# First batch's attention in one fixed order on three engines, with other counts of zero products and earlier raw weight words

## The chip, the core and the metric

The kernel runs on one core of one Trainium2 chip. The metric is the device time of one execution in microseconds (us), taken as the median of three runs. The engines are called as in the profile: PE is TensorE (matrix products), PEld its weight loads, DVE is VectorE, ACT is ScalarE, POOL is GpSimd, SP is SyncE, whose queue issues every DMA here.

## What is computed

The reference, cut to what matters, is a masked attention followed by two feed-forward blocks, all in float32 or better:

```python
scores = scale * np.matmul(q, k.transpose(0, 1, 3, 2))      # batch 4, heads 8, seq 576, head_dim 64
...
scores = np.where(masks[None, :, :, :], scores, -1000000000.0)   # window 32, or 128 with every 4th key
scores = scores - np.max(scores, axis=-1, keepdims=True)
attn = np.exp(scores)
attn = attn / (np.sum(attn, axis=-1, keepdims=True) + 1e-09)
x = np.matmul(attn, v)                                       # then 2304 tokens x 512
...
x = (x @ w_a) * (x @ w_b) @ w_out                            # 512 -> 1536 -> 512
h = x @ w_in                                                 # 512 -> 2048
return (np.maximum(h, 0.0) + alpha * np.minimum(h, 0.0)) @ w_out2
```

The weights come as float64 words.

## The kernel before, in words

**Steps.** The program is written as a row of steps. `step(products)` runs what the table `before` holds for this step, then the given products, then what the table `after` holds, then `convey()`, which moves every weight job on by one stage, then loads that were put off (`behind`). The steps are only the order in which the code is written. A scheduler then orders each engine's instructions, and may move one ahead of another that waits; only instructions given to `keep_in_program_order` hold their order, among them the DMA issues.

**The first batch.** Steps 0 to 16 (`n_start` = 17) are the attention of the first batch, one group of two heads and 192 queries for each of the steps 0 to 11. Group i has `scores` (PE into a bank `sp_i`), `largest` (DVE), `exps` (ACT), `weights` (DVE: sum, reciprocal, multiplication), `transposed` (PE into `tp_i`), `moved` (ACT copies `tp_i` to SBUF), `values` (PE into `ap_i`) and `placed` (ACT rounds `ap_i` into `xh`, DVE writes the rest into `xl`; what belongs to later token tiles is copied by DVE). `sp` has two banks, `tp` and `ap` one each.

**Zero products.** `heat(n)` issues n products of 128x512 zeros into a bank that nobody reads: 11 at the start, one in steps 0 to 2, and one in each of the steps 6 to 13.

**Weights.** A job of `convert` loads 512 KB of raw float64 words (`load_raw`, four places), waits two steps, makes float32 of them (two ACT instructions, L188 and L189, then one of DVE, L192, a step later) and splits the result into two parts another step later (`split`: ACT L266, DVE L269). Jobs are written here as a and the block and half (a00, a01, a10, a11, a20, a21, a30) for `w_a` and `w_b`, and o0, o1 for `w_out`. They begin at steps 5, 7, 9, 11, 13, 15 and then at every step from 17.

**The first feed-forward block.** From step 17 on, each block f of 128 hidden columns has three steps: `contract` into `pa` (12 products of 128x512), `contract` into `pb` (12 more), and the products of the block before with `w_out` into `accA`. Block 0 has banks `pa` and `pb`, block 1 the two called `acc`, block 2 `pa` and `pb` again. From step 20 on, groups of the second batch are put between these steps; their scores and values share banks called `sa`, and their queries and keys come by `load_qk(12)` and so on.

Of the kernel before, what the change touches and what calls it, by code (L numbers as in the profile page):

```python
# [62 lines left out]
def tile_kernel(ctx: ExitStack, tc: tile.TileContext, qk, v, mask, wab, wo1, w2, alpha, out):  # L63
# [143 lines left out]
    def convert(src, dest, then=None, raws=raw_ring, places=cf_ring):  # L207
# [7 lines left out]
        if then:  # L215
            then(f)
# [56 lines left out]
    def job_w(k, f, j):  # L273
        def dest():
            if j == 0:
                ws[f] = ws_places[f]
            return ws[f][:, 2 * j], ws[f][:, 2 * j + 1]

        def then(x):
            store_later(4 if now[0] < n_start else 2, wad[f, :, j * 512:(j + 1) * 512], x)  # L280

        queue.append((k, convert(wab[f, j], dest, then)))

    def job_o(k, f):
# [7 lines left out]
        queue.append((k, convert(wo1[f], dest, then)))  # L292
# [28 lines left out]
    class Group:  # L321


        def __init__(self, b, i, k=None, lag=None, tags=None):
# [5 lines left out]
            if k is None:  # L330
                return
            at_step(before, k, self.scores)
            at_step(after, k + lag[0], self.largest)
            at_step(after, k + lag[1], self.exps)
            at_step(after, k + lag[2], self.weights)
            at_step(before, k + lag[3], self.transposed)
            at_step(after, k + lag[3], self.moved)
            at_step(before, k + lag[4], self.values)
            at_step(after, k + lag[4], self.placed)
# [85 lines left out]
        def placed(self):  # L425

            base, p0, n = self.b * S, self.g * GS * QT, GS * QT
            if self.pr < 2:
                segs = [(0, n, base + p0, 1)]
            else:  # L430
                segs, p = [], p0
                while p < p0 + n:
                    r, m = divmod(p, NCLS)
                    e = min(p0 + n, (r + 1) * NCLS)
                    segs.append((p - p0, e - p, base + DILATION * m + r, DILATION))
                    p = e
            for o, n, t0, hop in segs:
                while n:
                    t = max(i for i, (first, _) in enumerate(TILES) if first <= t0)
                    k = min(n, (TILES[t][0] + TILES[t][1] - t0 + hop - 1) // hop)  # L440
                    c0 = t0 - TILES[t][0]
                    to, x = (slice(None), self.pr, slice(c0, c0 + (k - 1) * hop + 1, hop)), self.ap[:, o:o + k]
                    if t:
                        nc.vector.tensor_copy(xn[t][to], x)
                    else:
                        nc.scalar.copy(xh[to], x)
                        nc.vector.tensor_tensor(out=xl[to], in0=x, in1=xh[to].bitcast(F32), op=ALU.subtract)
                    o, n, t0 = o + k, n - k, t0 + k * hop
            self.ap = None
# [42 lines left out]
    def contract(acc, wh, wl, xh, xl, n):  # L492
        for c in range(NC):
            mm3(acc[:, :n], wh[:, c * 128:(c + 1) * 128], wl[:, c * 128:(c + 1) * 128],
                xh[:, c, :n], xl[:, c, :n], c == 0, c == NC - 1)
# [33 lines left out]

    nc.sync.dma_start(out=mk[:, 0:2], in_=mask[:, 0:2])  # L530
    load_qk(0)
# [19 lines left out]
    k = 5  # L551
    while due:
        job = min((x for x in due if n_start + x[1] <= k), default=None)
        if job:
            due.remove(job)
            if job[2] == "a":
                job_w(k, *job[3:])
            else:
                job_o(k, job[3])
        k += 2 if k < n_start else 1  # L560
# [198 lines left out]
    for t, (t0, n) in enumerate(TILES[:N_PLAIN]):  # L759
# [3 lines left out]
        for f in range(NFA):  # L763
# [5 lines left out]
            pa = bank("acc2" if early else "pa")  # L769
# [3 lines left out]
            step(lambda: contract(pa, wf[:, 0], wf[:, 1], xh, xl, n))  # L773
            pb = bank("acc3" if early else "pb")
# [3 lines left out]
            step(lambda: contract(pb, wf[:, 2], wf[:, 3], xh, xl, n))  # L778
# [7 lines left out]
            prev = (accs, wo_of(t, f), box, n, f, NFA, x1d, t)  # L786
        step(flush)
# [391 lines left out]
```

## Time and profile before

| what | us |
|---|---|
| median of three runs | 873.22 |
| lowest and highest of them | 872.21, 873.32 |
| the profiled execution | 876.13 |
| its span, first to last instruction | 874.4 |
| PE busy in the span | 862.3 (99%) |
| DVE busy, ACT busy | 622.0 (71%), 531.5 (61%) |
| mean granted clock of PE | 0.994 |

The span is the part of the profiled execution that the trace covers; the execution around it took 1.7 us more. A granted clock of 1.00 is 2.4 GHz, 0.50 is 1.2 GHz. PE is busy nearly all the time, so a change of the total can come from the stretches in which it is idle, works on what nobody reads, or has the lower clock.

### The profile page before, as it was taken

The page shows a single profiled execution, that of the slowest core. Times are in us where ns is not written, and L with a number is a line of the kernel's source. Part 1 is how long each engine was busy: PE and PEld are TensorE (multiplying, and loading weights), DVE is VectorE, ACT ScalarE, POOL GpSimd, SP SyncE. Part 2 cuts the span into 40 slices and gives each one's busy share as a digit, 9 for nine tenths or more (in the row PEclk, how much of TensorE's full clock was granted, in tenths as well). Part 3 has the DMA queues.
Part 4 walks back from the last instruction along what each step waited for, and adds up shares of the span by engine and source line. Part 5 has one row for each costly group of instructions (what it writes and reads, how often), then busy time and mean ns, then how long its engine had stood idle before and what let it go on. Part 6 is the DMA issues. An engine that isn't in the chain of part 4 may idle for free.

```text
span 874.4 us, 15617 instructions
## 1 busy us (share of the span) xinstructions
PE 862.3 (99%) x5417; PEld 782.1 (89%) x5422; DVE 622.0 (71%) x1438; ACT 531.5 (61%) x1183; POOL 0.7 (0%) x6
## 2 busy tenths in 40 slices
PE   8899999999999999999999999999999999999998
PEld 5578887888887888889999999999999999999998
DVE  5687674547657578969798737898575896557954
ACT  6798884556556566655553637775565855565542
POOL 0000000000000000000000000000000000000000
PEclk9799999999999999999999999999999999999999
DMA  9799984578789788999564559888887787788875
GB/s 256 232 326 358 321 291 156 195 247 276 238 311 324 260 288 278 324 319 316 195 229 167 179 218 312 263 237 263 277 252 240 251 270 225 227 250 258 270 223 184
DMA packets 106397, 225.28 MB, mean 258 GB/s; under 512 B 12112, under 2 KB 27216, under 8 KB 106320
## 3 DMA queue, kind: packets, MB, share of 16 engines
q1 hardware_dynamic: 106320, 224.30, 78.8%
q8 instruction: 43, 0.70, 0.3%
q14 instruction: 34, 0.28, 0.1%
HBM read 172.87 MB, written 51.38 MB: 256 GB/s over the span
## 4 chain that ended last, share of the span: by engine, by line
PE 91%; DMA 4%; DVE 2%; ACT 1%; issue 0%; SPq 0%; ACTq 0%; DVEq 0%
PE acc L1088 20%; PE at L795 12%; PE pb L795 8%; PE pa L795 8%; PE accA L488 4%; PE accA L489 4%; PE accA L490 4%; PE pb L488 4%; PE pa L488 4%; PE pb L490 4%; PE pb L489 4%; PE pa L490 4%; PE pa L489 4%; DMA wsd<-rt 2%; PE sa L416 2%; PE tp L403 2%
## 5 line engine op out<-in xcount | busy, mean ns | idle before, releaser
L269 DVE TENSOR_TENSOR rt<-ft,rt 128x512 fp32r<-128x512 f32 (+3 forms) x191 | 133.5, 705 | 78.7 <-ACT rt L266 77.8
L1088 PE MATMUL acc<-rt 128*128 128x384 f32 x1008 | 187.6, 334 | 0.0
L266 ACT CAST rt<-ft 128x512 fp32r<-128x512 f32 (+3 forms) x191 | 119.8, 633 | 97.6 <-DMA wsd<-rt 31.4
L1088 PEld LDWEIGHTS acc<-rt 128*128 128x128 f32 x1008 | 175.8, 188 | 0.4 <-ACT ft L1071 0.4
L795 PE MATMUL at<-rt 128*128 128x384 f32 x414 | 84.3, 335 | 0.0
L811 ACT COPY ft<-at 128x384 f32<-128x384 f32 x105 | 49.7, 474 | 51.9 <-PE at L795 51.4
L795 PEld LDWEIGHTS at<-rt 128*128 128x128 f32 x414 | 72.7, 188 | 0.4 <-ACT ft L811 0.3
L192 DVE SCALAR_TENSOR_TENSOR ft<-ft 128x512 uint32<-128x512 uint32 x68 | 46.7, 687 | 24.2 <-ACT ft L188 15.5
L488 PE MATMUL accA<-rt 128*128 128x512 f32 (+1 forms) x160 | 62.1, 391 | 0.6 <-DMA rt<-wod 0.6
L387 ACT ACTIVATE ft<-ft 128x96 f32<-128x96 f32 x144 | 52.3, 365 | 16.1 <-DVE ft L374 15.9
L489 PE MATMUL accA<-rt 128*128 128x512 f32 (+1 forms) x160 | 61.7, 386 | 0.0
L490 PE MATMUL accA<-rt 128*128 128x512 f32 (+1 forms) x160 | 61.5, 384 | 0.0
L269 DVE TENSOR_TENSOR rt<-gx,rt 128x768 fp32r<-128x768 f32 x43 | 41.1, 956 | 22.6 <-ACT rt L266 22.3
L189 ACT ACTIVATE ft<-ft 128x512 uint32<-128x512 uint32 x68 | 45.5, 672 | 18.8 <-DMA ft<-in_w 18.6
L795 PE MATMUL pb<-rt 128*128 128x384 f32 x276 | 55.8, 336 | 0.0
L795 PE MATMUL pa<-rt 128*128 128x384 f32 x276 | 55.3, 334 | 0.0
L795 PEld LDWEIGHTS pb<-rt 128*128 128x128 f32 x276 | 48.1, 188 | 1.1 <-DVE gx L808 0.5
L266 ACT CAST rt<-gx 128x768 fp32r<-128x768 f32 x43 | 36.0, 837 | 21.3 <-PE acc L1088 17.0
L795 PEld LDWEIGHTS pa<-rt 128*128 128x128 f32 x276 | 48.6, 188 | 0.0
L795 PE MATMUL at<-rt,rx 128*128 128x384 f32 x216 | 43.9, 336 | 1.6 <-ACT ft L811 1.6
L188 ACT ACTIVATE ft<-ft 128x512 f32<-128x512 f32 x68 | 45.2, 669 | 0.2
L266 ACT CAST rx<-ft 128x512 fp32r<-128x512 f32 (+1 forms) x58 | 32.4, 575 | 14.3 <-DVE ft L715 4.5
(148 smaller groups left out, 1705.1 us busy)
## 6 DMA issues: line engine op xcount, KB each, us to landing
rt<-wsd SPq DMA_DIRECT2D x318, 256.0 KB, 3.2
wsd<-rt SPq DMA_DIRECT2D x112, 256.0 KB, 4.8
ft<-in_w SPq DMA_DIRECT2D x32, 512.0 KB, 5.6
rt<-wod SPq DMA_DIRECT2D x31, 512.0 KB, 4.8
ft<-in_wab SPq DMA_DIRECT2D x24, 512.0 KB, 5.5
ft<-in_qk SPq DMA_DIRECT2D x48, 208.0 KB, 5.3
rx<-wod SPq DMA_DIRECT2D x17, 512.0 KB, 5.0
ft<-in_v SPq DMA_DIRECT2D x48, 144.0 KB, 5.4
```

Of the source, the lines that this page charges most:

```text
L188: held(nc.scalar.activation(f, high.bitcast(F32), AF.Prelu, scale=2.0 ** -112, alpha=-2.0 ** 32))
L189: nc.scalar.activation(low, low, AF.Copy, scale=0.933 * 2.0 ** -29)
L192: nc.vector.scalar_tensor_tensor(out=fi, in0=fi, scalar=3, in1=low, op0=ALU.logical_shift_left, op1=ALU.bitwise_or)
L266: hi_eng.copy(hi, x)
L269: lo_eng.tensor_tensor(out=lo, in0=x, in1=hi.bitcast(F32), op=ALU.subtract)
L387: nc.scalar.activation(self.et[:, s], self.st[:, s], AF.Exp, bias=self.sm[:, 0, s:s + 1], scale=-1.0, accum_out=self.sm[:, 1, s:s + 1])
L488: nc.tensor.matmul(acc, lhsT=wh, rhs=rh, start=first, stop=False)
L489: nc.tensor.matmul(acc, lhsT=wh, rhs=rl, start=False, stop=False)
L490: nc.tensor.matmul(acc, lhsT=wl, rhs=rh, start=False, stop=last)
L795: nc.tensor.matmul(acc[:, :HT], lhsT=a, rhs=x[:, b, c], start=start and c == k == 0, stop=c == 1 and k == 2, skip_group_check=not start,)
L811: nc.scalar.copy(out, acc[:, :HT])
L1088: nc.tensor.matmul(acc[a][:, :HT], lhsT=u, rhs=q[:, b, i % 2], start=new and first and k == 0, stop=last and k == 2, skip_group_check=not new,
```

## The change

Seven edits. (1) A function walks over the instructions of the stretch from the first zero product to the end of block 1's third step, and gives PE, ACT and DVE each an ordering dependence on the instruction written before it: within that stretch these three engines run in the order of the code. (2) The attention's stages are registered so that in step k PE has `sp_k`, `tp_(k-2)`, `ap_(k-3)`, in this order, and then the step's products. (3) `tp` and `ap` have two banks each. (4) Zero products: 5 at the start, 1 and 3 in steps 0 and 1, and 2 in each of the steps 2 to 11. (5) Block 0's `contract` is begun in steps 12 to 14, for the three quarters of the contraction that are there by then; steps 17 and 18 keep the last quarter. (6) Eight jobs instead of six begin before step 17, at other steps, and each has its own number of steps (`lead`) between the load and L188. (7) The first load is `load_qk(0)`, ahead of the mask; `placed` issues its ACT part for all pieces before the DVE part; the float weights are stored 3 steps after the split instead of 4.

```diff
-        yield
-        yield
+        for _ in range(lead):
+            yield
         for f in float_of(raw, places):
...
-            self.tags = tags
+            self.tags = [("at", 2), ("acc%d" % (3 * (i % 2)), 1), ("acc%d" % (1 + i % 2), 1)]
...
+    load_qk(0)
     nc.sync.dma_start(out=mk[:, 0:2], in_=mask[:, 0:2])
-    load_qk(0)
...
-    lag = (0, 0, 1, 2, 3)
-    for i in range(NC * NG):
-        Group(0, i, i, lag, [("at", 2), ("acc0", 1), ("acc1", 1)])
+    first = [Group(0, i) for i in range(NC * NG)]
+    stages = [(after, "largest", 0), (after, "weights", 1), (after, "moved", 2), (after, "placed", 3)]
+    stages += [(before, "scores", 0), (before, "transposed", 2), (before, "values", 3), (after, "exps", 0)]
...
-    k = 5
+    k, starts = 0, [(5, 2), (7, 2), (9, 4), (11, 3), (12, 3), (14, 2), (15, 2), (16, 2)]
     while due:
+        k, lead = starts.pop(0) if starts else (max(k + 1, n_start), 2)
...
-        k += 2 if k < n_start else 1
...
-    heat(11)
+    def in_source_order(first):
+
+        order = mybir.DependencyInfo(mybir.DependencyClass.NoSync, mybir.DependencyReason.DATA)
+        engines, last = [nc.tensor.engine, nc.scalar.engine, nc.vector.engine], {}
+        for n, ins in enumerate(nc.cur_bb.bb.instructions):
+            if n >= first and ins.engine in engines and ins.engine in last:
+                tc.add_manual_dep(ins, last[ins.engine].name, order, reason="in_source_order")
+            last[ins.engine] = ins
...
+        contract(begun[j], ws[0][:, 2 * j], ws[0][:, 2 * j + 1], xh, xl, 512, cs)
+
+    begins = len(nc.cur_bb.bb.instructions)
+    heat(5)
     for k in range(n_start):
-        if k < 3:
-            step(lambda: heat(1))
+        if k < 12:
+            step(lambda: heat((1, 3)[k] if k < 2 else 2))
+        elif k < 15:
+            step(lambda: [begin(*x) for x in (((0, 0),), ((0, 1),), ((0, 2), (1, 0, 1, 2)))[k - 12]])
         else:
-            step(lambda: heat(6 <= k < 14, tc.keep_in_program_order))
+            step()
...
+            cs = [NC - 1] if started else range(NC)
...
+            if (t, f) == (0, 1):
+                in_source_order(begins)
```

Three places show what that does to the order of instructions. Lines L349, L392 and L405 of the changed kernel are L360 (`scores`), L403 (`transposed`) and L416 (`values`) of the kernel before; L481 to L483 are L488 to L490 (`contract`), L268 is L269, L363 and L383 to L385 are L374 and L394 to L396.

PE at the end of the first batch, before (`sa_0` and `sa_1` are the scores of the second batch's first two groups, `pa` is block 0):

```order
L416 MATMUL ap_8_432<-ft 64x64 x6
L360 MATMUL sa_0_590<-ft 64x96 x3
L403 MATMUL tp_10_480<-ident,ft 96x128 x3
L568 LDWEIGHTS zeros
L568 MATMUL pb<-zeros 128x512
L360 MATMUL sa_0_590<-ft 64x96 x2
L488 MATMUL pa<-rt 128x512
L360 MATMUL sa_0_590<-ft 64x96
L489 MATMUL pa<-rt 128x512
L416 MATMUL ap_9_473<-ft 64x64 x6
```

PE at the same place in the changed kernel:

```order
L392 MATMUL tp_10_480<-ident,ft 96x128 x3
L405 MATMUL ap_9_484<-ft 64x64 x6
L481 MATMUL pa<-rt 128x512
L482 MATMUL pa<-rt 128x512
L483 MATMUL pa<-rt 128x512
L392 MATMUL tp_11_507<-ident,ft 96x128 x3
L405 MATMUL ap_10_511<-ft 64x64 x6
```

The second batch's scores were mixed with the end of the first batch; now the first batch ends with block 0's products between its groups, then come the rest of block 0 (18 products), all of `sa_0` and `sa_1`, and block 1.

DVE around the `weights` of group 11, before (`ap_8` is written by L447 and L444, the split of a weight job is L269):

```order
L447 TENSOR_TENSOR rt<-ap_8_432,rt 128x32
L444 COPY ft<-ap_8_432 128x16
L394 TENSOR_SCALAR ft<-ft 128x3
L447 TENSOR_TENSOR rt<-ap_8_432,rt 128x128
L444 COPY ft<-ap_8_432 128x16
L395 RECIPROCAL ft<-ft 128x3
L269 TENSOR_TENSOR rt<-ft,rt 128x512
L396 TENSOR_TENSOR ft<-ft 128x288
```

The same place in the changed kernel:

```order
L441 TENSOR_TENSOR rt<-ap_8_451,rt 128x32
L439 COPY ft<-ap_8_451 128x16
L441 TENSOR_TENSOR rt<-ap_8_451,rt 128x128
L439 COPY ft<-ap_8_451 128x16
L268 TENSOR_TENSOR rt<-ft,rt 128x512
L383 TENSOR_SCALAR ft<-ft 128x3
L384 RECIPROCAL ft<-ft 128x3
L385 TENSOR_TENSOR ft<-ft 128x288
```

The last three rows, the `weights` of group 11, now stand as one piece behind the split of job a01.

SP's queue where the second batch's queries and keys (`in_qk`) begin, before (`in_wab` and `in_wo` are raw words, `wad` is the store of float weights):

```order
L204 DMA ft<-in_wab 128x512
L314 DMA ft<-in_qk 128x416
L199 DMA wad<-ft 128x512
L204 DMA ft<-in_wo 128x512
L314 DMA ft<-in_qk 128x416 x2
L199 DMA wad<-ft 128x512
L204 DMA ft<-in_wab 128x512
L319 DMA ft<-in_v 96x384
```

The same place in the changed kernel:

```order
L199 DMA wad<-ft 128x512
L204 DMA ft<-in_wo 128x512
L313 DMA ft<-in_qk 128x416
L204 DMA ft<-in_wab 128x512
L313 DMA ft<-in_qk 128x416
L204 DMA ft<-in_wab 128x512
L313 DMA ft<-in_qk 128x416
L204 DMA ft<-in_wo 128x512
```

The second and third `in_qk` of the second batch stood right behind o0's load; now the loads of a21 and a30 stand ahead of them.

## Rows read from the trace of the kernel before

**Rows 1.** The page, its first line.
```profile
span 874.4 us, 15617 instructions
```

**Rows 2.** Windows: busy time of each engine, granted PE clock, DMA share, GB/s.
```profile
25.00:30.00 5.00, 3.29 (x29) 2.16 (x31) 3.99 (x19) 5.00 (x22) 0.00 (x0) 1.00 0.83 245
30.00:35.00 5.00, 3.88 (x31) 2.13 (x31) 3.19 (x11) 3.13 (x12) 0.00 (x0) 0.76 0.89 285
35.00:40.00 5.00, 5.00 (x28) 3.16 (x29) 2.01 (x5) 3.93 (x9) 0.00 (x0) 0.50 0.50 171
40.00:45.00 5.00, 5.00 (x28) 3.33 (x28) 2.98 (x7) 3.00 (x8) 0.00 (x0) 0.71 0.68 219
```

**Rows 3.** Windows, a later stretch, same columns.
```profile
60.00:200.00 140.00, 140.00 (x1005) 113.95 (x1004) 88.82 (x283) 96.67 (x240) 0.00 (x0) 1.00 0.78 266
```

**Rows 4.** Timeline of PE, the first batch: start, duration, instructions.
```profile
1.19 4.58 PE L568 MATMUL pb<-zeros 128*128 128x512 bf16 x11 [1.19 <-DVE zeros L563]
...
14.21 0.71 PE L360 MATMUL sp<-ft 64*64 64x96 f32 x12
14.85 0.39 PE L568 MATMUL pb<-zeros 128*128 128x512 bf16 x1
15.17 0.57 PE L416 MATMUL ap<-ft 96*64 96x64 f32 x12
15.67 0.53 PE L403 MATMUL tp<-ident,ft 128*96 128x128 f32 x3
16.13 0.71 PE L360 MATMUL sp<-ft 64*64 64x96 f32 x12
```

**Rows 5.** Timeline of PE, from the end of the first batch on.
```profile
31.38 0.54 PE L360 MATMUL sa<-ft 64*64 64x96 f32 x6 [0.97 <-DMA ft<-in_qk]
...
41.19 0.91 PE L416 MATMUL ap<-ft 96*64 96x64 f32 x12
...
51.29 0.39 PE L490 MATMUL acc<-rt 128*128 128x512 f32 x1
51.52 0.39 PE L488 MATMUL pa<-rt 128*128 128x512 f32 x1
...
61.40 0.73 PE L360 MATMUL sa<-ft 64*64 64x96 f32 x24
```

**Rows 6.** Timeline of ACT.
```profile
16.32 0.46 ACT L408 COPY ft<-tp 96x384 f32<-96x384 f32 x1
16.68 0.38 ACT L387 ACTIVATE ft<-ft 128x96 f32<-128x96 f32 x1
...
19.64 0.32 ACT L446 CAST rt<-ap 128x192 fp32r<-128x192 f32 x1 [0.15 <-PE ap L416]
...
20.95 0.67 ACT L188 ACTIVATE ft<-ft 128x512 f32<-128x512 f32 x1
21.53 0.65 ACT L189 ACTIVATE ft<-ft 128x512 uint32<-128x512 uint32 x1
...
26.17 0.62 ACT L266 CAST rt<-ft 128x512 fp32r<-128x512 f32 x1
```

**Rows 7.** Timeline of DVE.
```profile
27.11 0.69 DVE L269 TENSOR_TENSOR rt<-ft,rt 128x512 fp32r<-128x512 f32 x1
27.97 0.69 DVE L192 SCALAR_TENSOR_TENSOR ft<-ft 128x512 uint32<-128x512 uint32 x1 [0.18 <-ACT ft L189]
...
29.69 0.17 DVE L394 TENSOR_SCALAR ft<-ft 128x3 f32<-128x3 f32 x1
...
30.10 0.46 DVE L396 TENSOR_TENSOR ft<-ft 128x288 f32<-128x288 f32 x1
```

**Rows 8.** DMA, us to landing, issued at 1.17, 29.9 and 34.4 us.
```profile
ft<-in_qk SPq DMA_DIRECT2D x1, 208.0 KB, 2.5
...
ft<-in_qk SPq DMA_DIRECT2D x2, 208.0 KB, 5.4
...
ft<-in_wab SPq DMA_DIRECT2D x1, 512.0 KB, 4.3
```

More of the change, by code (lines that the diff above doesn't have):

```diff
@@ L214, in convert @@
         split(hi, lo, f, nc.scalar, nc.vector)
-        if then:
-            then(f)
+        then(f)
     def convert_s(which, i, raw_places, places, pace=1, lead=2):
@@ L271, in tile_kernel, with job_w @@
     ws, wo = {}, {}
-    def job_w(k, f, j):
+    def job_w(k, lead, f, j):
         def dest():
@@ L279, in then, with job_o @@
         def then(x):
-            store_later(4 if now[0] < n_start else 2, wad[f, :, j * 512:(j + 1) * 512], x)
-        queue.append((k, convert(wab[f, j], dest, then)))
-    def job_o(k, f):
+            store_later(3 if now[0] < n_start else 2, wad[f, :, j * 512:(j + 1) * 512], x)
+        queue.append((k, convert(wab[f, j], dest, then, lead)))
+    def job_o(k, lead, f):
         def dest():
@@ L290, in then @@
             store_later(2, wod[f], wo[0, f].rearrange("p h n -> p (h n)").bitcast(F32))
-        queue.append((k, convert(wo1[f], dest, then)))
+        queue.append((k, convert(wo1[f], dest, then, lead)))
     def reload_o(k, t, f):
@@ L321, in tile_kernel, with __init__ @@
     class Group:
-        def __init__(self, b, i, k=None, lag=None, tags=None):
+        def __init__(self, b, i):
             self.b, self.n, self.pr, self.g = b, b * NC * NG + i, i // NG, i % NG
             self.id = f"{b}_{i}"
-            self.tags = tags
+            self.tags = [("at", 2), ("acc%d" % (3 * (i % 2)), 1), ("acc%d" % (1 + i % 2), 1)]
             self.swap = 0
             self.shared = None
[L330 to L339, printed above, removed]
         def psum(self, n, what):
@@ L436, in placed @@
                     p = e
+            rest = []
             for o, n, t0, hop in segs:
@@ L442, in placed @@
                     to, x = (slice(None), self.pr, slice(c0, c0 + (k - 1) * hop + 1, hop)), self.ap[:, o:o + k]
-                    if t:
-                        nc.vector.tensor_copy(xn[t][to], x)
-                    else:
+                    if not t:
                         nc.scalar.copy(xh[to], x)
-                        nc.vector.tensor_tensor(out=xl[to], in0=x, in1=xh[to].bitcast(F32), op=ALU.subtract)
+                    rest.append((t, to, x))
                     o, n, t0 = o + k, n - k, t0 + k * hop
+            for t, to, x in rest:
+                if t:
+                    nc.vector.tensor_copy(xn[t][to], x)
+                else:
+                    nc.vector.tensor_tensor(out=xl[to], in0=x, in1=xh[to].bitcast(F32), op=ALU.subtract)
             self.ap = None
@@ L490, in mm3, with contract @@
         nc.tensor.matmul(acc, lhsT=wl, rhs=rh, start=False, stop=last)
-    def contract(acc, wh, wl, xh, xl, n):
-        for c in range(NC):
+    def contract(acc, wh, wl, xh, xl, n, cs=range(NC)):
+        for c in cs:
             mm3(acc[:, :n], wh[:, c * 128:(c + 1) * 128], wl[:, c * 128:(c + 1) * 128],
@@ L543, in tile_kernel @@
     at_step(after, 1, lambda: behind.append(lambda: nc.sync.dma_start(out=mk[:, 2:], in_=mask[:, 2:])))
-    lag = (0, 0, 1, 2, 3)
-    for i in range(NC * NG):
-        Group(0, i, i, lag, [("at", 2), ("acc0", 1), ("acc1", 1)])
+    first = [Group(0, i) for i in range(NC * NG)]
+    stages = [(after, "largest", 0), (after, "weights", 1), (after, "moved", 2), (after, "placed", 3)]
+    stages += [(before, "scores", 0), (before, "transposed", 2), (before, "values", 3), (after, "exps", 0)]
+    for k in range(NC * NG + 3):
+        for table, what, lag in stages:
+            if 0 <= k - lag < NC * NG:
+                at_step(table, k, getattr(first[k - lag], what))
     due = [(3 * f + j, -n_start, "a", f, j) for f in range(NFA) for j in range(2)]
     due += [(3 * f + 5, 3 * f - 3, "o", f, 0) for f in range(NFA)]
-    k = 5
+    k, starts = 0, [(5, 2), (7, 2), (9, 4), (11, 3), (12, 3), (14, 2), (15, 2), (16, 2)]
     while due:
+        k, lead = starts.pop(0) if starts else (max(k + 1, n_start), 2)
         job = min((x for x in due if n_start + x[1] <= k), default=None)
@@ L768, in tile_kernel @@
             early = (t, f) == (0, 1)
-            pa = bank("acc2" if early else "pa")
+            started = (t, f) == (0, 0)
+            cs = [NC - 1] if started else range(NC)
+            pa = begun[0] if started else bank("acc2" if early else "pa")
             g = g_tile(n)
@@ L772, in tile_kernel @@
             at_step(after, now[0] + 1, lambda g=g, pa=pa: nc.scalar.copy(g, pa[:, :n]))
-            step(lambda: contract(pa, wf[:, 0], wf[:, 1], xh, xl, n))
-            pb = bank("acc3" if early else "pb")
+            step(lambda: contract(pa, wf[:, 0], wf[:, 1], xh, xl, n, cs))
+            pb = begun[1] if started else bank("acc3" if early else "pb")
             k = now[0]
@@ L777, in tile_kernel @@
             at_step(after, k + 1 if final else k + 2, lambda g=g, box=box: split_g(box, g, n))
-            step(lambda: contract(pb, wf[:, 2], wf[:, 3], xh, xl, n))
+            step(lambda: contract(pb, wf[:, 2], wf[:, 3], xh, xl, n, cs))
             if final and t + 1 < N_PLAIN:
```

10 lines of the change are left out of this document (7 added, 3 removed).

## The prediction

> **What bounds the kernel now.** I read the page first, then the table of windows, then the timelines of PE, ACT and DVE up to 60 us, then the DMA issues. The span is 874.4 us [rows 1]; from 60 to 200 us PE is busy in all of 140 us at a granted clock of 1.00, while ACT is busy in 96.67 and the DMA share is 0.78 [rows 3]. There the end is set by PE alone. What can be won lies before that: from 25 to 30 us PE works for 3.29 of 5 us, from 30 to 35 for 3.88 while the clock falls, from 35 to 40 all the time but at 0.50, which is 1.2 GHz, and it is at the full level again only in the course of the slice from 40 to 45 [rows 2]. So I ask one thing: when does the first product of block 2 start? It starts at 51.52 [rows 5], with the first batch, blocks 0 and 1 (48 products of 128x512) and the first `sa` scores behind it. The same work lies behind it in the changed kernel, and what follows is PE's own rate in both, so the shift of that moment is the forecast.
>
> **The change, part by part.**
>
> *Zero products at the start, and the first load.* Eleven take 4.58 us, 0.42 each [rows 4]; five end at 1.19 + 2.1 = 3.3. `qk(0)` landed 2.5 us after its issue at 1.17 [rows 8]; issued some 0.4 earlier it lands at about 3.3. So `sp_0` starts 2.5 us sooner than the 5.77 at which the eleven end. Little of this remains: the next scores wait for their own loads, three more zero products follow in step 1, and `tp_0` needs largest, exps and weights of group 0. I take 9.0 for `sp_3`.
>
> *The cycle.* Before, a step is `sp` 0.64, one zero product 0.32, `ap` 0.50, `tp` 0.46, start to start: 1.92 [rows 4]. The second zero product follows the first directly; a 512-column product at the full level costs 0.23 from start to start (51.29 to 51.52) [rows 5]. So a step is 2.15, and `sp_7` starts at 9.0 + 4 x 2.15 = 17.6. The 0.23 is a loss in each step; nothing hides it, since PE is the one that sets the cycle here.
>
> *One order on three engines.* ACT's work in a step is three exps of about 0.37, the copy 0.36, casts of 0.2 to 0.3 [rows 6]: 1.7 us, below 2.15, so until step 7 ACT waits for PE. In step 7 ACT starts with `moved(5)` at 17.6 + 0.64 + 0.46 = 18.7. From there to the end of step 11 it has five steps, 8.5 us, plus L188 and L189 twice (0.58 + 0.56 each time) and L266 twice (0.52 to 0.55) [rows 6], 3.3 us together, and some 0.6 of waiting inside: 31.1. PE's five steps take 10.75, ACT's 12.4, and now nothing may step aside. The `weights` of group 11 stand on DVE behind the split of a01: 0.65 for it and 0.87 for sum, reciprocal and multiplication (29.69 to 30.10 and 0.46) [rows 7]. So `tp_11` cannot start before 31.1 + 0.1 + 0.65 + 0.87 = 32.7; I take 32.8. PE alone would reach it at 9.0 + 9 x 2.15 for the steps 3 to 11 and 1.65 for step 12 (`tp`, `ap` and three products), at 30.0: the fixed order costs 2.8 us here, which I expect as a wait of nearly 1 us before each of `tp_9`, `tp_10` and `tp_11`.
>
> *Block 0 begun early, nothing mixed in.* After `tp_11` PE has it (0.46), `ap_10` and `ap_11` (0.50 each), and from step 13 on 3 + 12 + 6 products at 0.23 (4.8): it is through at 32.8 + 6.3 = 39.1. The banks doubled for `tp` and `ap` remove waits that I don't see on the path, so I cost them at nothing; so too the ACT part of `placed` ahead of its DVE part and the store a step sooner.
>
> *The wait that the order of SP's queue adds.* `sa` needs `qk(12)` and `qk(13)`. The load of a21, the seventh, takes the raw place of a10, which is free when a10's L192 is done, and `qk(13)` stands behind it; behind that wait the load of a30, `qk(14)` and the load of o1. a10's L188 now comes in step 13: ACT copies `tp_11` to 33.7, casts `ap_10` to 34.1, L188 and L189 to 35.2, the casts of `ap_11` to 35.5; DVE has four short pieces to 36.0 and L192 (0.69 [rows 7]) to 36.7. a21 is issued then, `qk(13)` half a microsecond later. The bounds for its landing are 2.5, the load into an empty queue, and 5.4, the load under full traffic [rows 8]: 39.7 to 42.6. The nearest row is the 512 KB load into a half idle queue, 4.3 [rows 8], which here goes ahead; I take 3.9 for `qk(13)`, so 41.1. PE waits from 39.1 to 41.1. The Trainium skill, "DMA: Bandwidth & Descriptors", section "Anatomy of one DMA", gives a DMA a fixed 2.0 us plus its bytes over 436 GB/s, fitted on another issue path; by this estimate the 720 KB are there 3.7 us after a21's issue, at 40.4, and the sum would be 0.7 us lower.
>
> *The rest.* `sa` is 24 products in 0.7 [rows 5], block 1 is 24 x 0.23 = 5.5. Block 2 starts at 41.1 + 0.6 + 5.5 = 47.2. Its weights are no later: a20 is split before 42; a21's words land at 41.1 (36.8 + 4.3), ACT needs 1.1 for them and DVE and ACT some 3 more, and block 2's second half starts at 50.
>
> **Sum.** 51.5 - 47.2 = 4.3 us sooner. The profiled execution took 876.13 with its span of 874.4, 2.9 us over the median of 873.22; the 4.3 comes off either. The forecast for the median is 868.9. Without the uncertain waits, its own range is 866.7 to 870.9 (block 2 at 45 to 49, by the bounds for `qk(13)` and by 1 us of error in ACT's chain).
>
> **The rivals.**
>
> *The orders cost nothing.* If ACT, DVE and the load keep up, PE's own work sets block 2: `sp_11` at 26.2, then 2.15, two steps of 1.65, 0.5, 18 products (4.1), 0.7 and 5.5: 42.5, 9 us sooner, 864.2. Against it stands ACT's 12.4 us in 10.75. Chance 0.06.
>
> *The clock still falls late.* Before, PE was busy 3.29 of 5 us and then waited for `qk` for 0.97 [rows 5] when it fell [rows 2]. In the changed kernel the waits before `tp_9` to `tp_11` and before `sa` make a similar stretch. From `tp_11` on PE then needs up to twice 6.3 us: `ap` is 0.91 at the low level against 0.57 [rows 4, 5]. Two of the 6.3 are absorbed by the wait for `qk(13)`: 3.5 us lost, 872.4. For it: the gaps. Against it: two products of zeros and six of block 0 lie among the first three waits, and 15 more of block 0 ahead of the last. Chance 0.18.
>
> *The low level stays from the start, and the kernel is slower.* The eleven products ahead of `sp_0` took 0.42 each, which is 512 columns at 1.2 GHz [rows 4]. With five, then scores mixed with single zeros, the engine may stay at 1.2 GHz. A step then costs 2.15 times 1.6 (`ap`) to 1.85 (a long product), 3.4 to 4.0. Nine steps from 3 to 11 are 11 to 17 us more, of which the 4 us of waits absorb a part: 880, and it decides from three steps on (3 x 1.5 is the gain). For it: from 35 to 40 us PE was busy without a break with scores, values, transposes and some products, and its clock stayed at 0.50 [rows 2]. Against it: from 1.2 to 5 the changed PE is full too, and half of that is zero products. The Trainium skill's "TensorE: Matmul & The Clock Gate", Part 1, says "the default state is throttled, and activity releases the throttle"; by this rule fewer products at the start are a risk, and the slice from 35 to 40 us agrees in so far as the level stayed low beside full occupation. Chance 0.18.
>
> *It is given back later.* If the stage from 50 us on were bound by the conversions or the DMA, 873.2 would remain. But the DMA share is 0.78 and ACT 69% from 60 to 200 [rows 3], and the loads run ahead as before. Chance 0.08.
>
> **The numbers.** The forecast has the chance 0.50. A difference under 0.2%, 1.75 us, is about what cannot be told from none. Faster: 0.50, 0.06, and a third of the late fall, 0.06: 0.62. Same: the other 0.12 and most of the last rival: 0.19. Slower: the low level from the start, and a little: 0.19. The range runs from 865.5, which takes in most of the sum's lower error, to 876, which takes in the late fall and a low level of a few steps; the long low level and the first rival are left out.
>
> **What would show it.** `sp_0` at 3.3 and `sp_11` at about 26; PE idle for about 1 us before each of `tp_9` to `tp_11`; a wait of PE for `in_qk` of some 2 us before `sa`; clock 1.00 in all slices from 5 to 50; block 2 at 47. It is wrong if zero products after 8 us last 0.43, if the clock drops between 30 and 42, or if PE idles for weights after 47.

## The result and the profile after

The changed kernel took 879.97 us (median of 5 runs, 877.49 to 881.93), the kernel before beside it 873.32 (5 runs, 872.21 to 876.48). The ratio is 1.0066, 95% interval 1.0036 to 1.0095: slower by 0.66%, where 868.9 was forecast. The profiled execution took 881.93 with a span of 880.1 [rows 1].

The windows of the changed kernel (busy time of PE, PEld, DVE, ACT, POOL, then granted PE clock, DMA share, GB/s), which answer [rows 2, 3]:

```profile
25.00:30.00 5.00, 3.91 (x57) 2.55 (x56) 4.45 (x27) 5.00 (x22) 0.00 (x0) 1.00 0.84 285
30.00:35.00 5.00, 3.80 (x43) 2.24 (x43) 4.44 (x22) 3.70 (x17) 0.00 (x0) 1.00 0.60 199
35.00:40.00 5.00, 5.00 (x42) 3.87 (x38) 2.63 (x10) 4.65 (x12) 0.00 (x0) 1.00 0.17 33
40.00:45.00 5.00, 3.56 (x36) 2.57 (x35) 3.13 (x5) 4.55 (x9) 0.00 (x0) 1.00 0.94 288
45.00:50.00 5.00, 5.00 (x24) 4.14 (x23) 1.89 (x3) 0.79 (x2) 0.00 (x0) 1.00 0.96 346
...
60.00:70.00 10.00, 9.43 (x71) 7.12 (x70) 8.59 (x27) 9.89 (x27) 0.00 (x0) 0.66 1.01 350
60.00:200.00 140.00, 139.43 (x950) 113.23 (x949) 88.33 (x282) 95.01 (x240) 0.00 (x0) 0.98 0.76 261
```

The stretch at 0.50 between 33 and 43 us is gone, as forecast. Two new things stand there: from 35 to 40 us the DMA engines are nearly idle (0.17), and from 45 to 50 us ACT works for only 0.79 of 5 us. A fall of the clock follows, later than any forecast looked: 0.66 over 60 to 70 us. This profiled execution is the slowest of the five, so its sizes need not be those of the median one.

PE's timeline of the changed kernel, to be read beside [rows 4, 5]:

```profile
3.43 1.23 PE L349 MATMUL sp<-ft 64*64 64x96 f32 x12
...
8.74 1.22 PE L349 MATMUL sp<-ft 64*64 64x96 f32 x12
...
10.79 0.71 PE L349 MATMUL sp<-ft 64*64 64x96 f32 x12
...
28.23 0.71 PE L349 MATMUL sp<-ft 64*64 64x96 f32 x12
...
29.71 0.50 PE L392 MATMUL tp<-ident,ft 128*96 128x128 f32 x3 [0.78 <-ACT ft L376]
...
32.14 0.50 PE L392 MATMUL tp<-ident,ft 128*96 128x128 f32 x3 [0.89 <-DVE ft L385]
...
42.82 0.71 PE L349 MATMUL sa<-ft 64*64 64x96 f32 x20 [1.44 <-DMA ft<-in_qk]
...
49.03 0.39 PE L481 MATMUL pa<-rt 128*128 128x512 f32 x1
...
53.79 0.51 PE L481 MATMUL accA<-rt 128*128 128x512 f32 x1 [0.94 <-ACT rt L265]
...
59.63 0.51 PE L392 MATMUL tp<-ident,ft 128*96 128x128 f32 x3 [1.62 <-DVE ft L385]
60.71 0.56 PE L392 MATMUL tp<-ident,ft 128*96 128x128 f32 x3 [0.57 <-DVE ft L385]
...
66.47 0.63 PE L483 MATMUL accA<-rt 128*128 128x512 f32 x1
...
74.85 0.82 PE L392 MATMUL tp<-ident,ft 128*96 128x128 f32 x6
```

`sp_0` (3.43), `sp_3` (10.79), `sp_11` (28.23), the waits before `tp_9` and `tp_10`, the wait for `in_qk` before `sa`: down to block 2's first product at 49.03, all that was forecast is there, 1.8 us late. Then come an idle time for a split (L265), two before the next transposes, and from 61 to 68 us products that start 0.43 apart instead of 0.23. The last row, the six transposes (L392) of the second batch's second pair of groups, is my mark in what follows, since behind it, from 75 to 200 us, PE is busy in all of 125 us in every kernel here. In the first profile of before it lies at 70.36, so the changed kernel is 4.5 us behind there, and 5.7 us at the end of the span. The mark is no exact measure: in three profiles of the kernel before (two of them below) the span ends 804.0, 807.0 and 805.1 us behind it.

What ACT waits for from 45 to 50 us is in its timeline of the changed kernel:

```profile
35.66 0.66 ACT L188 ACTIVATE ft<-ft 128x512 f32<-128x512 f32 x1
...
44.70 0.62 ACT L265 CAST rt<-ft 128x512 fp32r<-128x512 f32 x1
49.52 0.66 ACT L188 ACTIVATE ft<-ft 128x512 f32<-128x512 f32 x1 [4.21 <-DMA wad<-ft]
...
50.63 0.60 ACT L265 CAST rt<-ft 128x512 fp32r<-128x512 f32 x1
```

The L188 at 49.52 is that of a30, the eighth job. The ring of float words has five places; jobs 6, 7 and 8 take those of a00, a01 and a10, and a10's words are still to be stored (`wad`). Why that store is late stands in SP's timeline of the changed kernel:

```profile
31.56 0.45 SPq L313 DMA_DIRECT2D ft<-in_qk  x1
38.63 0.33 SPq L204 DMA_DIRECT2D ft<-in_wab  x1
...
43.44 0.50 SPq L199 DMA_DIRECT2D wad<-ft  x1
```

SP issues nothing from 32.0 to 38.6 us: the load of a21 waits for a10's raw place, which is free only when a10 is converted, and a10's L188 is at 35.66. Behind it stand two loads of queries and keys, the raw words of a30 and o1, a load of values and a10's store; each of the raw loads waits for its own place again, so the store comes last, at 43.44, with the others still on the way. The DMA view of the changed kernel (bytes of one, then us from issue to landing) shows the store of 43.44 us:

```profile
wad<-ft SPq DMA_DIRECT2D x1, 256.0 KB, 6.0
```

It is on the way until 49.4, and ACT starts again at 49.52. What ACT still owed then is what PE waits for: the split of block 0's product (its use with `w_out` is block 1's third step), behind a21's split in ACT's order, at 53.79, and the exps of the second batch, done only at 59.5, at 59.63.

### The profile page after: what moved, and what is told of

The parts are those of the page before. It is cut to its first block, busy times and chain, and to the rows that moved or that the text cites. A ratio compares the mean times of both kernels' runs of the same rounds, so it can differ in the third digit from the quotient of the medians.

```text
span 880.1 us, 15622 instructions
## 1 busy us (share of the span) xinstructions
PE 863.5 (98%) x5424; PEld 782.2 (89%) x5429; DVE 622.3 (71%) x1438; ACT 531.5 (60%) x1183; POOL 0.7 (0%) x6
## 4 chain that ended last, share of the span: by engine, by line
PE 78%; DMA 10%; DVE 5%; ACT 4%; issue 2%; SPq 1%; ACTq 0%; DVEq 0%
PE acc L1109 20%; PE at L816 11%; PE pb L816 7%; PE pa L816 7%; DMA wsd<-rt 4%; PE accA L481 4%; PE accA L482 3%; PE accA L483 3%; PE pa L481 3%; PE pa L482 3%; PE pa L483 3%; PE pb L481 2%; PE pb L482 2%; PE pb L483 2%; DMA ft<-in_w 2%
## 5 line engine op out<-in xcount | busy, mean ns | idle before, releaser
L268 DVE TENSOR_TENSOR rt<-ft,rt 128x512 fp32r<-128x512 f32 (+3 forms) x191 | 133.6, 706 | 88.0 <-ACT rt L265 87.4
L265 ACT CAST rt<-ft 128x512 fp32r<-128x512 f32 (+3 forms) x191 | 119.1, 633 | 94.8 <-DMA wsd<-rt 30.7
L481 PE MATMUL accA<-rt 128*128 128x512 f32 (+1 forms) x160 | 63.8, 399 | 2.7 <-DMA rt<-wod 1.7
L482 PE MATMUL accA<-rt 128*128 128x512 f32 (+1 forms) x160 | 62.5, 390 | 0.1
L192 DVE SCALAR_TENSOR_TENSOR ft<-ft 128x512 uint32<-128x512 uint32 x68 | 46.6, 687 | 22.4 <-ACT ft L188 17.2
L483 PE MATMUL accA<-rt 128*128 128x512 f32 (+1 forms) x160 | 62.0, 387 | 0.0
L268 DVE TENSOR_TENSOR rt<-gx,rt 128x768 fp32r<-128x768 f32 x43 | 41.1, 957 | 22.3 <-ACT rt L265 22.1
L265 ACT CAST rt<-gx 128x768 fp32r<-128x768 f32 x43 | 36.0, 837 | 20.9 <-PE acc L1109 16.9
L188 ACT ACTIVATE ft<-ft 128x512 f32<-128x512 f32 x68 | 45.3, 668 | 5.2 <-DMA wad<-ft 4.2
L265 ACT CAST rx<-ft 128x512 fp32r<-128x512 f32 (+1 forms) x58 | 32.4, 575 | 13.9 <-DVE ft L732 4.7
```

What stands on the lines that cost most here:

```text
L188: held(nc.scalar.activation(f, high.bitcast(F32), AF.Prelu, scale=2.0 ** -112, alpha=-2.0 ** 32))
L192: nc.vector.scalar_tensor_tensor(out=fi, in0=fi, scalar=3, in1=low, op0=ALU.logical_shift_left, op1=ALU.bitwise_or)
L265: hi_eng.copy(hi, x)
L268: lo_eng.tensor_tensor(out=lo, in0=x, in1=hi.bitcast(F32), op=ALU.subtract)
L481: nc.tensor.matmul(acc, lhsT=wh, rhs=rh, start=first, stop=False)
L482: nc.tensor.matmul(acc, lhsT=wh, rhs=rl, start=False, stop=False)
```

## The experiments

The first theory (A): the late store of a10, by its hold on a float place, stops ACT, and the gaps behind it bring PE's clock down. Rivals: (B) the fixed order itself, since nothing may step aside; (C) the low level in the first 10 us; (D) the base: the long stretch at 0.50 in the profile of before is not in every execution, so there was less to win. Ratios are to the kernel before on the same chip, with 95% intervals.

**The order taken away**, all else as changed.

```diff
-            if (t, f) == (0, 1):
-                in_source_order(begins)
```

> The changed kernel without the fixed order on PE, ACT and DVE; all else as changed. Theory A (the float store of job a10 is issued late and lands late, and ACT's L188 of job a30, which reuses its place, waits 4.2 us for it with everything else of ACT behind it): the store stays late, so most of the loss stays, about 877. Theory B (the fixed order itself costs the time, because ACT and DVE may not step aside): at most 873, PE without idle time from 50 to 62 us. Theory C (the low clock at the start and again at 61 us is the loss by itself): no change of more than 1 us, about 879.

Measured: 879.89, 1.0065 (1.0043 to 1.0087). The store costs ACT only 0.18 here and PE is busy from 35 to 60 us. The first batch ends later (`sp_11` 30.36), with SP's queue standing from 34.7 to 39.5; block 2 starts at 51.88, but only because twelve `accA` products now stand ahead of it, which begin at 49.16. Three rows of its PE timeline, the last of them the first half of the mark:

```profile
60.40 0.71 PE L349 MATMUL sa<-ft 64*64 64x96 f32 x12
...
63.09 0.71 PE L349 MATMUL sa<-ft 64*64 64x96 f32 x12
...
69.10 0.49 PE L392 MATMUL tp<-ident,ft 128*96 128x128 f32 x3
```

The same scores, of a later pair of groups, in the changed kernel:

```profile
113.90 0.73 PE L349 MATMUL sa<-ft 64*64 64x96 f32 x24
```

At the mark this kernel is 5.8 us ahead of the changed one, at a granted clock of 1.00, so all but 1 us of what the changed kernel loses between 49 and 75 us is gone with the order. The time is lost behind the mark instead: the scores of a pair of groups, 24 products in 0.73 us in the changed kernel, run here as two pieces of 0.71, and the values as two of 0.57 instead of one of 0.92. It is so for the first five pairs, up to 130 us, and their values then start 17.2 us apart (92.61, 109.81, 127.01) instead of 16.0 (81.06, 97.06, 113.06). So the edit changed more than the order. That the median comes out the same is chance, and this run doesn't decide on B.

**The order only up to step 16.**

```diff
-            if (t, f) == (0, 1):
-                in_source_order(begins)
...
+    in_source_order(begins)
     at_step(after, start_of[1], lambda: tc.keep_in_program_order(nc.sync.dma_start(out=al, in_=alpha)))
```

> The fixed order ends with step 16, so only the first batch and the begun products have it. Theory A: a30's L188 still waits for the store, but the exps of the second batch need not stand behind it: 875 to 878. Theory B: 871 to 873, since the first batch keeps its gain and the rest is free again. Theory C: about 879.

Measured: 878.64, 1.0048 (1.0025 to 1.0071), block 2 at 48.54; its interval holds the 1.0066 of the changed kernel, and the second batch's first pairs run in single pieces here too (0.71 and 0.71 from 57.51 and 60.21), so it decides little. What decides on B is the run with other starts below, which keeps the order.

**Float places of their own for jobs 6 to 9**, so that none waits for a store.

```diff
     cf_ring = Ring(ft, 8192, 512, 5)
+    once_f = cf_ring.places + Ring(ft, 0, 512, 4).places
...
-        f = places.next()
+        f = once_f.pop(0) if places is cf_ring and once_f else places.next()
```

> Jobs 6 to 9 get float places of their own, so that a30 doesn't reuse a10's; the fixed order stays. Theory A: ACT waits less than 0.5 us before a30's L188, PE is not idle from 50 to 61 us, the clock doesn't fall at 61, and the time is 870 to 872. Theory B: 877 to 880. Theory C: 878 to 880.

Measured: 877.35, 1.0047 (1.0021 to 1.0073). The wait for the store is gone, but ACT now waits for the raw words themselves (0.58, 1.29, 0.41 us) and PE idles 1.32 at 49.71: a wait that was covered by the other. A had forecast 870 to 872 here; the result is not told apart from the changed kernel.

**Float weights stored one step behind the split instead of three.**

```diff
-            store_later(3 if now[0] < n_start else 2, wad[f, :, j * 512:(j + 1) * 512], x)
+            store_later(1 if now[0] < n_start else 2, wad[f, :, j * 512:(j + 1) * 512], x)
```

> The float weights of the early jobs are stored 1 step after the split instead of 3, so that a10's store stands ahead of a30's load in SP's queue. Theory A: it is issued near 39.5 us and lands by 43, and the time is 870 to 872.5, as with the places. Theory B: 877 to 880. Theory C: 878 to 880.

Measured: 876.33, 1.0024 (1.0003 to 1.0046). The store of a10 is issued at 37.50 instead of 43.44; ACT's timeline in this kernel:

```profile
43.96 0.69 ACT L188 ACTIVATE ft<-ft 128x512 f32<-128x512 f32 x1 [0.62 <-DMA ft<-in_wab]
...
46.90 0.66 ACT L188 ACTIVATE ft<-ft 128x512 f32<-128x512 f32 x1 [1.19 <-DMA ft<-in_wo]
...
50.01 0.69 ACT L188 ACTIVATE ft<-ft 128x512 f32<-128x512 f32 x1 [0.87 <-DMA wad<-ft]
```

The wait of 4.21 is down to waits of about 1, the clock doesn't fall at 61 us, the mark is at 68.41. A carries a part of the loss, by the medians 3.6 of the 6.65 us (the two intervals overlap from 1.0036 to 1.0046); it had forecast 870 to 872.5, which would be all of it.

**The kernel before once more, twice**, unchanged, for D.

> The kernel before once more, for a second profile. Theory D (the clock's fall near 33 us is not in every execution of the kernel before, so its profile is one of its slower executions and its median has less to win back): this profile has no fall between 25 and 45 us, or a shorter one, block 2 starts 2 to 5 us before 51.5, and the run takes 871 to 874. Rival: every execution has the fall at about the same place; block 2 starts within 1 us of 51.5 and the run takes 873 to 877.

> The same once more, since one execution says little on how often the clock falls: theory D gives at least one of the two profiles without the fall of the first one; the rival gives both with it.

Measured: 874.11 and 872.81. Windows of the second of these profiles:

```profile
25.00:30.00 5.00, 4.40 (x24) 3.27 (x24) 4.27 (x20) 4.07 (x18) 0.00 (x0) 0.66 0.93 318
30.00:35.00 5.00, 4.41 (x47) 2.71 (x47) 2.98 (x10) 4.16 (x15) 0.00 (x0) 1.00 0.56 193
```

and two lines of its PE timeline:

```profile
47.01 0.39 PE L488 MATMUL pa<-rt 128*128 128x512 f32 x1
...
65.88 0.81 PE L403 MATMUL tp<-ident,ft 128*96 128x128 f32 x6
```

In both the clock falls at 26 us, for 3.4 us instead of 10.2, and block 2 starts at 46.41 and 47.01, not at 51.52 [rows 5]; the mark is at 65.26 and 65.88. D holds, though not for all of these 5 us: the spans are 872.3 and 871.0, which is 2.1 and 3.4 under the first profile's 874.4.

**Eleven zero products at the start again**, for C.

```diff
-    heat(5)
+    heat(11)
```

> The changed kernel with 11 zero products at the start instead of 5. Theory C (the low level of the start is what costs): PE has the full level by 6 us, sp_3 starts near 9 to 9.5 instead of 10.8, and up to 2 us come back, 877.5 to 878.5. Theory A: what the start wins waits in front of the same store, and the time is within 1 us of the changed kernel's 880.

Measured: 878.88, 1.0059 (1.0031 to 1.0088); `sp_11` comes 0.8 sooner (27.41), block 2 0.9, but the gaps behind it (0.67, 1.62, 0.57) and a fall at 60 us (0.83 over 60 to 70) are as in the changed kernel. C is worth about 1 us by the medians, which the intervals don't tell from nothing.

**The sooner stores, queries and keys a step sooner, and eleven zero products, together.**

```diff
-    heat(5)
+    heat(11)
...
-            store_later(3 if now[0] < n_start else 2, wad[f, :, j * 512:(j + 1) * 512], x)
+            store_later(1 if now[0] < n_start else 2, wad[f, :, j * 512:(j + 1) * 512], x)
```

and `load_qk(i)` of the second batch put off to step i + 1 instead of i + 2.

> Three mends of the changed kernel together: stores 1 step after the split, the second batch's queries and keys asked for one step sooner (so that the second stands ahead of a21's load), 11 zero products at the start. Theory A: PE's wait for in_qk before sa (1.4 to 1.8 us) goes, nothing takes its place, and the time is 873.5 to 875.5, 1 to 3 us under the run with the stores alone (876.3). Theory B (the order of the three engines costs by itself): no better than 876.

Measured: 875.86, 1.0026 (1.0008 to 1.0043). The wait before `sa` is gone and block 2 is at 45.99, sooner than in any profile of before, yet PE then idles 1.19, 0.59 and 0.57 for splits and transposes, and the mark is at 68.68. Mending single waits doesn't bring the time back; something further ahead makes them all.

**One part undone: the starts and leads of the weight jobs.** SP's queue stood still for a raw place that a longer lead holds (a10 has lead 4), so this was the next theory (E).

```diff
-    k, starts = 0, [(5, 2), (7, 2), (9, 4), (11, 3), (12, 3), (14, 2), (15, 2), (16, 2)]
+    k, starts = 0, [(5, 2), (7, 2), (9, 2), (11, 2), (13, 2), (15, 2)]
```

> The changed kernel with one part undone: the weight jobs begin at steps 5, 7, 9, 11, 13, 15 and from 17 on, as before, with a lead of 2. If the early raw words are what costs (they pull the eighth job onto a float place whose store is late, and pile up the loads after 38 us), the wait of ACT for the store of a10 is gone, and the median is 874 to 876.5. If they are needed for the earlier blocks (rival), PE idles for the weights of blocks 1 and 2 by 2 us and more, and the median is 879 to 884.

Measured: 872.55, 0.9981 (0.9958 to 1.0003): the whole loss is gone. SP's timeline of this kernel:

```profile
30.17 0.42 SPq L313 DMA_DIRECT2D ft<-in_qk  x1
33.94 0.33 SPq L199 DMA_DIRECT2D wad<-ft  x1
34.32 1.96 SPq L313 DMA_DIRECT2D ft<-in_qk  x1
36.38 0.38 SPq L204 DMA_DIRECT2D ft<-in_wab  x1
```

PE's:

```profile
8.91 0.71 PE L349 MATMUL sp<-ft 64*64 64x96 f32 x12
...
30.27 0.50 PE L392 MATMUL tp<-ident,ft 128*96 128x128 f32 x3 [0.89 <-DVE ft L385]
...
39.14 0.72 PE L349 MATMUL sa<-ft 64*64 64x96 f32 x24
...
50.14 0.51 PE L392 MATMUL tp<-ident,ft 128*96 128x128 f32 x3 [0.28 <-DVE ft L385]
...
64.69 0.82 PE L392 MATMUL tp<-ident,ft 128*96 128x128 f32 x6
```

a10's L188 is at 30.71 in this kernel, and now the queries and keys stand ahead of a21's load: `sa` runs without a wait, PE's one gap between it and the mark is 0.28, and the mark is 10.2 us ahead of that of the changed kernel (1.9 of them already at `sp_3`, ahead of every weight job). The waits of the fixed order before `tp_10` are the same 0.89 as there, so they are not what was lost. This kernel has the fixed order and loses nothing by its median, so B alone isn't the cause.

**One zero product a step instead of two**, in the kernel with the three edits above.

```diff
-            step(lambda: heat((1, 3)[k] if k < 2 else 2))
+            step(lambda: heat((1, 3)[k] if k < 2 else 1))
```

> The kernel with the earlier stores, the earlier queries and keys and eleven zero products at the start (875.86), now with one zero product in the steps 2 to 11 instead of two. If the second product sets the cycle of PE and nothing else does, ten steps are 2.3 us shorter, sp_11 starts at about 25 instead of 27, and the median is 873.5. If ACT's chain or the weights set the end of the first batch (rival), sp_11 comes sooner but block 2 does not (45.5 to 46.5), and the median stays at 875 to 876. If the second product is what holds the full level, the clock falls between 25 and 40 us, and the median is 877 to 880.

Measured: 876.35, 1.0032 (1.0014 to 1.0050). `sp_11` starts at 25.58 instead of 26.94 in the kernel it was made from, but the clock falls, as its windows show:

```profile
25.00:30.00 5.00, 2.64 (x43) 1.90 (x40) 4.72 (x27) 4.97 (x22) 0.00 (x0) 1.00 0.35 120
30.00:35.00 5.00, 4.70 (x36) 2.92 (x33) 2.73 (x12) 3.02 (x9) 0.00 (x0) 0.69 0.83 288
35.00:40.00 5.00, 5.00 (x25) 3.96 (x25) 2.56 (x7) 3.56 (x9) 0.00 (x0) 0.63 0.19 42
```

PE works 2.64 of 5 us and then goes at the low level: the second product does hold the level here, and the ten executions bear it out: mean clocks of 0.994 to 1.00 with one, 0.999 and 1.00 with two. The median, 876.35 against 875.86, does not tell the two apart.

**The second zero product alone**, in the kernel before, steps 6 to 13.

```diff
-            step(lambda: heat(6 <= k < 14, tc.keep_in_program_order))
+            step(lambda: heat(2 * (6 <= k < 14), tc.keep_in_program_order))
```

> The kernel before with one part alone: two zero products instead of one in each of the steps 6 to 13. If they hold the full level through the end of the first batch, the fall at 26 us (3.4 us at 0.50 in two profiles of before, 10.2 in the first) is gone, and the median is 871 to 872.5. If the gaps decide and not the products (rival), the fall stays and the eight products cost 0.23 each: 873.5 to 875.

Measured: 873.90, 1.0011 (0.9995 to 1.0027). The granted clock is 1.00 in all its slices from 5 to 70 us, and nothing is won: the mark is at 66.44, against 65.26 and 65.88. What the fall of 3.4 us cost, the extra products and the waits of 1.25, 0.46 and 0.76 cost too.

**All leads 2, the starts as changed**, to part the two halves of E.

```diff
-    k, starts = 0, [(5, 2), (7, 2), (9, 4), (11, 3), (12, 3), (14, 2), (15, 2), (16, 2)]
+    k, starts = 0, [(5, 2), (7, 2), (9, 2), (11, 2), (12, 2), (14, 2), (15, 2), (16, 2)]
```

> The changed kernel with the same starts of the weight jobs (5, 7, 9, 11, 12, 14, 15, 16), but a lead of 2 steps for all of them. If the longer leads make the loss, by holding the raw places and with them SP's queue, the load of a21 is issued by 34 us instead of 38.6, ACT does not wait for the store of a10, and the median is 872 to 875. If the earlier loads make it (rival), the eighth job still finds its float place in the store queue or its words late, and the median is 877 to 880.

Measured: 875.02, 1.0004 (0.9986 to 1.0022). a21's load is issued at 34.37 instead of 38.63, and ACT's waits for stores are short:

```profile
46.94 0.66 ACT L188 ACTIVATE ft<-ft 128x512 f32<-128x512 f32 x1 [1.30 <-DMA wad<-ft]
...
49.37 0.67 ACT L188 ACTIVATE ft<-ft 128x512 f32<-128x512 f32 x1 [0.20 <-DMA wad<-ft]
```

The mark is at 67.75, 7.1 us ahead of the changed kernel's, 1.5 of them from `sp_3` on (9.28 against 10.79): the leads make 5.6 of the 8.3 us that the kernel without starts and leads won behind `sp_3`, the earlier starts the rest (PE still idles 1.17 for a split at 48.70). By the medians it is 5.0 of 7.4.

**The starts and leads alone, in the kernel before.** `convert` and the two functions that queue a job get the lead as in the change, and the list of starts is that of the change.

```diff
-    k = 5
+    k, starts = 0, [(5, 2), (7, 2), (9, 4), (11, 3), (12, 3), (14, 2), (15, 2), (16, 2)]
     while due:
+        k, lead = starts.pop(0) if starts else (max(k + 1, n_start), 2)
```

> The kernel before with one part alone: the starts and leads of the weight jobs from the change. If they make the loss by themselves, SP's queue stands still for 5 us and more after 30 us, block 2 starts at 48 or later, and the median is 877 to 880. If they need the fixed order and the zero products to make it (rival), the scheduler moves other work ahead and the median stays at 872 to 875.

Measured: 874.84, 1.0010 (0.9996 to 1.0024). By its steps the eighth job writes its float words at step 18 into the place that a10's store reads at step 19, so what it stores is not a10's words, later token tiles load wrong weights for that half, and the wait in question is not in the program. Hence one more:

**The same with the store three steps behind the split.**

```diff
-            store_later(4 if now[0] < n_start else 2, wad[f, :, j * 512:(j + 1) * 512], x)
+            store_later(3 if now[0] < n_start else 2, wad[f, :, j * 512:(j + 1) * 512], x)
```

> The kernel before with two parts of the change: the starts and leads of the weight jobs, and the store of the float weights three steps behind the split. If starts and store make the loss without the fixed order, ACT or PE waits for the store of a10 or for weights between 45 and 60 us, and the median is 877 to 880. If the fixed order and the zero products are needed too (rival), it stays at 873 to 876, as the run with the starts alone did.

Measured: 874.60, 1.0017 (1.0000 to 1.0034). Neither ACT nor PE waits for a store of float words up to 60 us; PE's longest wait behind 31 us is 0.27. So the starts and leads cost at most little by themselves (1.5 us by the medians); with the rest of the change, undoing them gives back 7.4.

**Starts and leads undone, and the stores sooner**, in search of a version that beats both.

```diff
-    k, starts = 0, [(5, 2), (7, 2), (9, 4), (11, 3), (12, 3), (14, 2), (15, 2), (16, 2)]
+    k, starts = 0, [(5, 2), (7, 2), (9, 2), (11, 2), (13, 2), (15, 2)]
...
-            store_later(3 if now[0] < n_start else 2, wad[f, :, j * 512:(j + 1) * 512], x)
+            store_later(1 if now[0] < n_start else 2, wad[f, :, j * 512:(j + 1) * 512], x)
```

> The changed kernel without the early starts (872.55), with the early float stores one step behind the split instead of three. If stores sooner free places that are still waited for, the median is 870.5 to 872. If nothing waits for them any more (rival), it stays at 872 to 873.5, or loses by holding SP's queue for the split.

Measured: 874.69, 1.0013 (0.9994 to 1.0032), no gain on 872.55. In SP's timeline of this kernel the sooner stores themselves hold the queue, for 4.5 and 4.3 us:

```profile
25.37 0.38 SPq L318 DMA_DIRECT2D ft<-in_v  x1
30.33 0.33 SPq L199 DMA_DIRECT2D wad<-ft  x1
30.75 0.38 SPq L204 DMA_DIRECT2D ft<-in_wab  x1
35.44 0.33 SPq L199 DMA_DIRECT2D wad<-ft  x1
```

The same edit that gave 3.6 us in the changed kernel gives nothing here, and `sa` waits 0.85 for its keys again.

## Why the prediction was wrong

**The gain was taken off the wrong base.** "The 4.3 comes off either" failed first. The profiled execution had a clock of 0.994 and 876.13 us. Of 115 executions of the kernel before that stood beside these runs, 21 had a mean clock of 0.994 or less (median 877.1), 83 one of 0.997 or more (median 872.7). The median of 873.22 lies with the second kind, where, by the two further profiles, block 2 starts at about 46.7 already; the forecast of 47.2 for the changed kernel, had it been exact, would have left the median about where it was. The 4.3 us were there to be won in about one execution in five. That the profiled execution lay 2.9 us over the median, and over the highest run shown, was in the text, and I didn't ask where those 2.9 us were.

**"What follows is PE's own rate in both" failed next**, with "its weights are no later" under it, and this made the kernel slower. I followed the load of a21 behind a10's L192 in SP's queue, and took the wait before `sa` from it (2 us forecast, 1.44 measured). I stopped there. The same wait held a10's store, that store held a float place, and in ACT's fixed order a21's split stood behind the L188 that needed it: it came at 50.63, where the forecast's steps put it near 45. Block 2's second half still began right behind its first, at 51.75; what PE idled for stood behind a21's split, block 0's split and the exps. From block 2's first product to the mark the changed kernel takes 74.85 - 49.03 = 25.8 us, before 65.88 - 47.01 = 18.9 (second profile): 6.9 us, of which the idle times at 53.79, 59.63 and 60.71 are 0.94 + 1.62 + 0.57 = 3.1, and the low level from 61 to 68 us, by the clock of 0.66 over 10 us, 3.4. Undoing the leads and starts takes all this away, the leads alone most of it. That the store's wait is part of the chain is borne out by the sooner store (3.6 us back by the medians). That the clock fell because of the gaps is argued from their order and not shown: the kernel with the three edits idled 1.19, 0.59 and 0.57 us in the same stretch and stayed at 1.00. Nor does a loss of this size need the fall: the ten executions without the order had mean clocks of 0.999 and 1.00 and the same median, with the time lost in the pairs' single pieces.

**The steps up to block 2 held, but for one size.** The cycle is 2.14 to 2.15 as forecast; ACT's and DVE's chain makes `tp_11` late as worked out (waits of 0.78, 0.89 and 0.32 where nearly 1 each was said; 34.35 against 32.8). The start was mis-sized: `sp_3` at 10.79 instead of 9.0, because the first scores still took 1.22 and `sp_1` waited 1.00 for its load. This 1.8 us is all by which block 2 misses its 47.2. With the same instructions up to there, other kernels had `sp_3` at 8.91 and 9.28, so 9.0 is a start that some executions reach and the profiled one did not. A slip besides: block 2 at 49 gives 870.7, not the 870.9 of the sum's upper end.

**The rivals.** "It is given back later" had 0.08, with the argument that the loads run ahead as before from 50 us on; it was nearest to what happened, only that the stage between 43 and 60 us, not the later one, gave it back, and more than was won. "The low level stays from the start" forecast a slower kernel by another mechanism: its 880 is near 879.97, but the scores take 0.71, their full rate, from 10.79 on, the granted clock is 1.00 up to 60 us, and eleven zero products give 1 us at most. The slice from 35 to 40 us of the kernel before, counted there as agreeing with the sentence quoted from the Trainium skill, agrees only with its first half: PE was busy in all of it and the level stayed at 0.50. "The clock still falls" was looked for at `tp_9` to `sa`, where it didn't come. For the Trainium skill, "DMA: Bandwidth & Descriptors", "Anatomy of one DMA", whose 2.0 us plus bytes over 436 GB/s (fitted on another issue path) stood in the prediction: by this estimate a21's words and `qk(13)`, 720 KB, are there 3.7 us after the first issue, and the rows give 4.2 (38.63 to 42.8); for the 256 KB store it gives 2.6, and the row shows 6.0, behind the loads issued in the 5 us ahead of it; so for the store the trace disagrees.

**What stays open.** Why the kernel without the order ends its first batch 2.1 us later than with it, and why it takes the second batch's pairs apart, which the kernel before, without any such order, doesn't. How much of the loss the median execution of the changed kernel has in each stretch: its mean clocks run from 0.994 to 0.998. And whether the change without its starts and leads beats the kernel before: 0.9981 reaches to 1.0003.

## What to carry to other kernels

A gain read from one profile counts only as far as the executions behind the median have the stretch it removes: when the profiled time is over the highest run, look first for what it has that they lack. When a load waits for a place in an in-order queue, list everything behind it, the stores too, and for each store who next writes its source; with a fixed order on the engine that writes, one late store stops all of that engine's work. A longer wait between a load and its conversion isn't free: it holds the load's place for just as long. And an experiment that frees a scheduler changes more than the stretch in question: compare the stretches behind it too before the two times are compared.

## What the runs showed of the hardware

The same first instructions run at different rates. The scores of step 1 started behind nearly the same wait in the kernel with the sooner stores and in the one with starts and leads undone and sooner stores:

```profile
5.71 0.71 PE L349 MATMUL sp<-ft 64*64 64x96 f32 x12 [0.51 <-DMA ft<-in_qk]
```

```profile
5.69 1.23 PE L349 MATMUL sp<-ft 64*64 64x96 f32 x12 [0.50 <-DMA ft<-in_qk]
```

They took 0.71 and 1.23 us, while the granted clock of both reads 1.00 for the slice from 5 to 10 us; so that column does not show the slow start, the durations do. Scores of two groups cost hardly more than those of one where they run as one piece: 0.73 us for 24 products, 0.71 for 12. A 256 KB store of float words landed in 2.3 to 3.8 us when issued between 25 and 43 us in the first profile of before (five stores), and in 6.0 and 6.5 when issued at 43.44 and 45.42 in the changed kernel, where the queue had stood still for 6.6 us and then made eleven issues in 8 us.
